# Score pairs spread among a step's products, in a two-layer attention and mixer kernel

## The chip, the cores and the metric

The kernel runs on one core of a Trainium2 chip. The metric is the device time of one execution in microseconds, the median over several runs. The engines are TensorE (PE in the profile, with its weight loads as PEld), VectorE (DVE), ScalarE (ACT), GpSimd (POOL) and SyncE (SP, which only issues DMAs here). TensorE writes to PSUM alone; DVE and ACT clear PSUM into SBUF, and POOL and the DMAs work on SBUF.

## The reference

For each of 8 batches, with 3200 rows, 256 columns of `v` and `u` and 64 of `z`:

```python
scores = (1.0 / S) * z @ z.T                 # 3200 x 3200
attn   = maximum(scores, 0) ** 2
x      = u * (attn @ v)                      # 3200 x 256

wq, wk = x @ w_q, x @ w_k                    # 3200 x 64
mixed  = (1 / sqrt(64)) * (wq @ wk.T) @ x    # computed as wq @ (wk.T @ x)
out    = maximum(mixed, 0) @ w_out
```

## The kernel before

**Tiles and groups.** A batch's 3200 rows are 25 tiles of 128. The output rows of the attention are worked on in seven groups: six of 512 rows and a last one of 128. A *score* is a tile of keys against a group: one matmul of 64 rows (`z` has 64 columns) by 512 columns. Two of them make a *pair*, one in the lower 64 partitions of the array and one in the upper, which run side by side, into one PSUM tile `sc` of two banks (`scores`, L275). Each pair is cleared by one instruction, `relu` and a scale into `g` (`first_stage`: DVE L289 or ACT L287), and squared by another into `at` in 16 bits (`second_stage`: ACT L298 or POOL L300). Scores are symmetric, so some `at` tiles are transposed by DMA (L317) into `tt` and serve a second group.

**Products.** The sum over keys of `at` against `v` goes to two PSUM banks, `acc0` and `acc1`, each holding two of a group's four row tiles (`second_product`). Its 128 key rows are also cut into two *lanes*, the lower and the upper 64 partitions. In pass one the lower lane works on one bank and the upper lane on the other; in pass two they have changed banks, so that two lanes never write one bank at once (`lanes`, L333 through `Item.emit`). Between the passes stands `swap_after`: a nop on TensorE that waits for the last matmul of each lane of pass one. `evened` pads a shorter lane with zeros. The last group of a batch but the last is *split*: it has one row tile, each lane has a bank for itself, and it needs no swap (`both_lanes`).

**Steps.** The main loop (`while groups`) runs 171 steps. A step scores up to three pairs, squares those of the step before (`waiting`), and multiplies some of the rows that were scored two steps before or kept from earlier. A step may *begin* a group (its accumulators start) or *close* it: then `gate` multiplies the sums with `u` (ACT copies one bank, L441; DVE takes the other, L442; POOL finishes, L444), and SP transposes the result for the mixer. Between the groups' work come pieces of the mixer: a step may *mix* (two matmuls `mx` at its head and two pairs in place of three), carry *keys* (`qk`: projections and heads), or a *projection* (`fo`, 512 output rows, then stored).

**Where the pairs stand.** A step that begins a group scores all its pairs at its head, but one less where it carries keys or a projection. Another step scores one pair at its head, or none where it mixes. The other pairs are `between_`: the program issues them all between the two passes, after the second squaring of ACT, ahead of the nop of the swap:

```python
firsts = [lanes(part, across, False) for part in parts]
...
for x in acts[1:]:
    second_stage(*x)
for p0 in between_:
    stage(p0, scores(p0))
...
for part, ends_ in zip(parts, firsts):
    swap_after(ends_)
    lanes(part, across, True)
```

Where a middle or closing step carries keys or a projection, pass one is: half of the products, the extra's first pass, the other half; then come the later pairs, the swap and second pass of the extra, and the swap and second pass of the products. In a beginning step the extra stands first.

**What orders the work.** The order is written out by hand: each engine takes its instructions in the order in which this loop issues them, and semaphores alone make them wait. The second pair of a step is cleared by ACT (the first in the step after a group's end), the others by DVE; in a step that mixes ACT clears the mix and DVE both pairs. Of the pairs of the step before, POOL squares the first, ACT the second, and a third is ACT's in even steps and POOL's in odd ones. PSUM tiles for `sc`, `mx`, `qk` and `fo` come from one pool of three (`pps`), `g` from seven.

Of the kernel before, what the change touches and what calls it, by code (L numbers as in the profile page):

```python
# [16 lines left out]
def kernel(  # L17
# [218 lines left out]
    for b in range(B):  # L236
        for gi in range(NG):
# [7 lines left out]
            else:  # L245
                odd = len(tiles) % 2
                order, rest = own[:odd], own[odd:]
                n_, m_ = len(near) // 2, (len(rest) + 1) // 2
                at_ = sorted(
                    [((i + 0.5) / max(n_, 1), near[2 * i : 2 * i + 2]) for i in range(n_)]  # L250
                    + [((i + 0.7) / max(m_, 1), rest[2 * i : 2 * i + 2]) for i in range(m_)]
                )
# [11 lines left out]
    def scores(p0):  # L264
        pair = tiles[p0 : p0 + 2]
        sc = ps_tile("sc")
        ats = [[], []]
        for h, (b, gi, tis) in enumerate(pair):
            w = widths[gi]
            half = h * dqk  # L270
            for i in range(W // w):
                ti = tis[min(i, len(tis) - 1)]
                ats[h].append((i * w, h, w, b, ti, starts[gi], half))
        for at, h, w, b, ti, gs, half in sorted(ats[0] + ats[1]):
            nc.tensor.matmul(  # L275
                out=sc[:, h, at : at + w],
                lhsT=zT[b][half : half + dqk, ds(z_at(b, h) + ti * P, P)],
                rhs=zT[b][half : half + dqk, ds(z_at(b, h) + gs, w)],
                start=True,
                stop=True,  # L280
            )
        return sc
# [11 lines left out]
    def second_stage(p0, g, on_act):  # L294
        at = pat.tile([P, 2 * W], FP16, tag="at", name="at")
        out = at[:].rearrange("p (a w) -> p a w", a=2)
        if on_act:
            nc.scalar.square(out=out, in_=g[:])  # L298
        else:
            nc.gpsimd.tensor_mul(out=out, in0=g[:], in1=g[:])  # L300
        blocks = []
        for h, (b, gi, tis) in enumerate(tiles[p0 : p0 + 2]):
            for i, ti in enumerate(tis):
                made[b, gi, ti] = (at, h * W + i * widths[gi])
            gj = group_of(tis[0])
            if is_turned(gi, gj):
                blocks.append((b, gi, gj, tis[0] - starts[gj] // P, 1, h * W, (h + 1) * W))
        if len(blocks) == 2 and blocks[0][:3] == blocks[1][:3] and blocks[1][3] == blocks[0][3] + 1:
            blocks = [blocks[0][:4] + (2, blocks[0][5], blocks[1][6])]
        for b, gi, gj, n0, nn, c0, c1 in blocks:  # L310
            if (b, gi, gj) not in turned:
                bufs = {1: 3, 2: 4, 4: 1}[gj - gi]
                turned[b, gi, gj] = ptt.tile(
                    [P, 4, 4, P], FP16, tag=f"tt{gj - gi}", name=f"tt{gj - gi}", bufs=bufs
                )
            out = turned[b, gi, gj][:].rearrange("p n j t -> p (n j) t")
            nc.sync.dma_start_transpose(out=out[:, 4 * n0 : 4 * (n0 + nn), :], in_=at[:, c0:c1])  # L317
# [7 lines left out]
    ALL, LOW, HIGH = slice(0, P), slice(0, P // 2), slice(P // 2, P)  # L325

    class Item:
# [4 lines left out]
        def emit(self, rows, start, stop):  # L332
            return nc.tensor.matmul(  # L333
                out=self.out, lhsT=self.lhsT(rows), rhs=self.rhs(rows), start=start, stop=stop
            )
# [6 lines left out]
    def width(i):  # L342
        n = 1
        for d in i.out.shape[1:]:
            n *= d
        return n
# [12 lines left out]
            items[-1:-1] = [z_] * (n // D or 1)  # L359
        return items  # L360

    def lanes(banks, across, second):
        todo, ends_ = [], {}
        for lane, rows in enumerate((LOW, HIGH)):
            at = 0
            for i in evened(banks, lane ^ across):
                todo.append((at, lane, i, rows))
                at += width(i)
        for _, lane, i, rows in sorted(todo, key=lambda x: x[:2]):
            ends_[lane] = i.emit(rows, i.start and not second, i.stop and second)  # L370
        return list(ends_.values())

    def both_lanes(banks):
        for low, high in zip(*banks):
            low.emit(LOW, low.start, low.stop)
            high.emit(HIGH, high.start, high.stop)

    def swap_after(ends_):
        ins = nc.tensor.nop()
        for earlier in ends_:  # L380
            tc.add_manual_dep(
                ins.ins,
                earlier.ins.name,
                mybir.DependencyInfo(mybir.DependencyClass.Sync, mybir.DependencyReason.DATA),
                reason="the lanes change banks",
            )
# [133 lines left out]
    def spread_heads(b):  # L520
        nc.scalar.copy(out=hss[b][dh:P, :], in_=hss[b][0:dh, :])
        nc.scalar.copy(out=hz[b % 2][dh:P, :], in_=hss[b][0:dh, :])
# [165 lines left out]
    keyed, keyed_at, to_turn, to_spread, asides = [], [-9], [], [], []  # L688
# [124 lines left out]
    def key_due(k):  # L813
# [10 lines left out]
            return False  # L824
        return since > 2

    made_by = []
    waiting = []
    produced = consumed = k = 0
    groups = [(b, gi) for b in range(B) for gi in range(NG)]  # L830
    left, steps, across = None, 0, False
    gate_pending = False
    while groups:
# [3 lines left out]
        n = 4 if k == 0 else 6  # L837
        mixing = None
# [6 lines left out]
        if mix_due(k):  # L845
            mixing = todo_mix.pop(0)
            mixed_at[0] = k
            mixing += (mix(*mixing),)
            n = 4
        n = min(n, NTILE - produced)  # L850
        pairs = list(range(produced, produced + n, 2))
        on_lanes = k >= 3 and len(pairs) + bool(mixing) >= 2
        keying = not mixing and key_due(k)
        begins = left is None
        projecting = not keying and todo_proj and groups[0] != (last, LASTG) and (
            begins or len(todo_proj) > 2 or len(groups) <= NG
        )
        heading = len(pairs)
        if on_lanes:
            heading = heading - bool(keying or projecting) if begins else 1 - bool(mixing)  # L860
        between_ = pairs[heading:]
        pairs = pairs[:heading]
        fresh = [(p0, scores(p0)) for p0 in pairs]
# [7 lines left out]
        def stage(p0, sc):  # L871
            on_act = len(staged) == act_pair and not mixing
            staged.append((p0, first_stage(p0, sc, on_act)))
# [15 lines left out]
        acts = [x for x in seconds if x[2]]  # L889
# [14 lines left out]
        b, gi = groups[0]  # L904
# [16 lines left out]
        closes = steps == 1  # L921
# [5 lines left out]
        rows_ = [t for _, _, tis in tiles[consumed : consumed + new] for t in tis]  # L927
# [7 lines left out]
        extra = None  # L935
# [6 lines left out]
        if on_lanes:  # L942
            split = is_split(b, gi)
            if extra and not all(extra[0]):
                for fn in whole(extra[0]):
                    fn()
                extra[1]()
                extra = None
            parts = [] if split else [banks]
            if extra and not begins and not split:  # L950
                n_ = len(banks[0]) // 2
                parts = [[bank[:n_] for bank in banks], extra[0], [bank[n_:] for bank in banks]]
            elif extra:
                parts.insert(0, extra[0])
            cut = len(rows_) // 4
            firsts = [lanes(part, across, False) for part in parts]
            if len(parts) == 3:
                parts, firsts = [extra[0], banks], firsts[1:]
            if split:
                both_lanes([bank[:cut] for bank in banks])  # L960
            for x in acts[1:]:
                second_stage(*x)
            for p0 in between_:
                stage(p0, scores(p0))
            if parts:
                across = not across
            for part, ends_ in zip(parts, firsts):
                swap_after(ends_)
                lanes(part, across, True)
                if extra and part is extra[0]:  # L970
                    extra[1]()
            if split:
                both_lanes([bank[cut:] for bank in banks])
        else:
            assert not is_split(b, gi)
            matmuls = whole(banks)
            cut = 10 if extra else 0
            if closes and (b, gi) == (last, LASTG):
                assert not extra
                cut = 20  # L980
                psg = [acc_tile(1, "xtx")[:, 0:D], ps_tile("xtx")[:, 0, 0:D]]
                extra = [], lambda: last_gram(last, LASTG - 1, psg)
            for fn in matmuls[:cut]:
                fn()
            if extra:
                for fn in whole(extra[0]):
                    fn()
                extra[1]()
            for x in acts[1:]:
                second_stage(*x)  # L990
            for fn in matmuls[cut:]:
                fn()
# [5 lines left out]
            left = None  # L998
        while to_spread:
            spread_heads(to_spread.pop(0))  # L1000
        waiting = staged
        k += 1

# [85 lines left out]
```

## Time and profile before

| | |
|---|---|
| runs | 799.5, 800.5, 802.95 us; median 800.5 |
| the profiled execution | 801.4 us |
| its span, first to last instruction | 799.6 us |
| mean granted TensorE clock | 0.997 |
| PE, PEld busy | 97%, 86% |
| DVE, ACT, POOL busy | 58%, 70%, 69% |
| DMA | 147.03 MB, 184 GB/s in the mean |

A row of the profile's groups names the line, the engine, the operation, the tiles written and read, their shapes and the count; then the busy time of the group, the mean of one in ns, the idle time of the engine just before them, and who ended most of it. A row of the timeline gives the start, the length, the engine and line, and in brackets the idle time of the engine ahead of it with its releaser; equal instructions that follow one another are merged (x24). A row of the waits gives who waited for whom, us in total, how many times and the longest. Ends of matmuls are modelled: one of 256 columns lasts 0.27 us in the records, though the next in its lane starts 0.11 us after it, so idle time of PE shorter than that does not show as idle.

### The profile page before, as it was taken

Reading aid. Unit: us, or ns where it says so; the run is one execution under the profiler, and the core shown is the slowest. Engines: PE = TensorE matmul, PEld = TensorE weight load, DVE = VectorE, ACT = ScalarE, POOL = GpSimd, SP = SyncE. Lnnn points to the kernel's source line nnn. Section 1 sums busy time; section 2 is a strip of 40 time slices with the busy share of each in tenths; the row PEclk is TensorE's granted clock in tenths of the full one; section 3 lists DMA queues with packets and bytes.
Section 4 is the critical chain, followed back from the end, with each engine's and each line's share of the span. In section 5 each row is a group of like instructions: output and inputs, shape, how many; then the busy total and the mean of one; then the engine's idle time right before and its main releaser. Section 6 shows DMA issues by size and latency. Waiting matters only on the chain. (4 is left out here: it accounts for less than half of the span.)

```text
span 799.6 us, 28394 instructions
## 1 busy us (share of the span) xinstructions
PE 773.6 (97%) x12590; PEld 683.9 (86%) x12590; DVE 465.8 (58%) x455; ACT 559.7 (70%) x656; POOL 553.2 (69%) x364
## 2 busy tenths in 40 slices
PE   7999999999999999999989999999999999999996
PEld 4878879998899988999879997999988898887984
DVE  5755576556655557455746457655575556664434
ACT  6776777877768776676767667758686877574565
POOL 7888698768666677765959658985677536866350
PEclk9999999999999999999999999999999999999999
DMA  8999799975999579994799949899499994987526
GB/s 156 179 218 200 132 204 185 189 178 121 211 218 203 126 181 210 207 241 128 172 212 228 225 123 165 230 187 256 119 207 200 220 222 94 187 186 162 157 58 256
DMA packets 276266, 147.03 MB, mean 184 GB/s; under 512 B 252080, under 2 KB 255664, under 8 KB 276144
## 3 DMA queue, kind: packets, MB, share of 16 engines
q1 hardware_dynamic: 275424, 143.33, 83.7%
q0 software_dynamic: 576, 1.64, 1.2%
q8 instruction: 98, 1.61, 0.8%
q14 instruction: 24, 0.20, 0.1%
q10 hardware_dynamic: 144, 0.26, 0.1%
HBM read 59.38 MB, written 26.21 MB: 107 GB/s over the span
## 5 line engine op out<-in xcount | busy, mean ns | idle before, releaser
L289 DVE TENSOR_SCALAR g<-sc 128x1024 f32<-128x1024 f32 x338 | 405.7, 1221 | 281.2 <-PE sc L275 253.0
L333 PE MATMUL acc<-v_sb,at 64*128 64x256 f16 (+1 forms) x7387 | 481.0, 270 | 3.6 <-POOL at L300 1.6
L300 POOL TENSOR_TENSOR at<-g 128x1024 f16<-128x1024 f32 x239 | 447.2, 1894 | 35.5 <-DVE g L289 35.3
L333 PEld LDWEIGHTS <-at 64*128 64x128 f16 (+1 forms) x7387 | 405.4, 94 | 51.0 <-issue 6.3
L298 ACT ACTIVATE at<-g 128x1024 f16<-128x1024 f32 x229 | 235.1, 1054 | 39.0 <-DVE g L289 38.1
L287 ACT ACTIVATE g<-sc 128x1024 f32<-128x1024 f32 x130 | 133.2, 1025 | 78.5 <-PE sc L275 77.0
L444 POOL TENSOR_TENSOR x_sb<-gt,u_sb 128x512 f16<-128x512 f32 x48 | 61.2, 1275 | 178.1 <-ACT gt L441 172.0
L333 PE MATMUL acc<-v_sb,tt 64*128 64x256 f16 (+1 forms) x2540 | 180.6, 269 | 0.0
L275 PE MATMUL sc<-zT 64*128 64x512 f16 (+1 forms) x1104 | 161.0, 347 | 5.6 <-ACT g L287 3.3
L333 PEld LDWEIGHTS <-tt 64*128 64x128 f16 (+1 forms) x2540 | 142.5, 94 | 3.3
L275 PEld LDWEIGHTS <-zT 64*128 64x128 f16 x1104 | 63.4, 94 | 14.7 <-issue 9.4
L578 ACT ACTIVATE rt<-mx 128x1024 f16<-128x1024 f32 x47 | 47.9, 1025 | 24.5 <-PE mx L557 22.5
L333 PE MATMUL fo<-wo,rt 64*128 64x256 f16 (+1 forms) x688 | 58.6, 271 | 2.2 <-DVE g L289 1.3
L639 ACT ACTIVATE fo<-fo 128x1024 f32<-128x1024 f32 (+2 forms) x44 | 43.6, 999 | 20.7 <-PE fo L333 20.4
L333 PE MATMUL qk<-x_sb,kx 64*128 64x256 f16 x368 | 54.6, 269 | 2.1 <-DVE g L289 2.0
L333 PEld LDWEIGHTS <-rt 64*128 64x128 f16 (+1 forms) x688 | 42.5, 95 | 14.7 <-issue 6.5
L441 ACT COPY gt<-acc 128x512 f32<-128x512 f32 x48 | 28.2, 587 | 31.3 <-PE acc L333 30.9
L442 DVE TENSOR_TENSOR x_sb<-acc,u_sb 128x512 f16<-128x512 f32 x48 | 33.1, 689 | 20.5 <-PE acc L333 18.4
L333 PEld LDWEIGHTS <-kx 64*128 64x128 f16 (+1 forms) x386 | 36.0, 94 | 7.1 <-DMA kx<-ql 0.9
L333 PE MATMUL qk<-xT_sb,wkq 64*128 64x512 f16 (+1 forms) x90 | 31.6, 376 | 1.0 <-DMA xT_sb<-x_sb 1.0
L479 ACT CAST qk<-qk 128x512 f16<-128x512 f32 x47 | 27.3, 582 | 7.1 <-PE qk L333 7.0
L333 PE MATMUL qk<-xT_sb,wqk 64*128 64x512 f16 (+1 forms) x94 | 30.0, 377 | 0.0
(79 smaller groups left out, 260.4 us busy)
## 6 DMA issues: line engine op xcount, KB each, us to landing
u_sb<-in_u_dram SPq DMA_DIRECT2D x48, 512.0 KB, 5.1
out_dram<-fo SPq DMA_DIRECT2D x45, 512.0 KB, 3.5
piece<-in_v_dram SPq DMA_DIRECT2D x42, 512.0 KB, 4.7
piece<-in_z_dram SPq DMA_DIRECT2D x7, 512.0 KB, 5.6
tt<-at SPq DMA_TRANSPOSE x162, 5.1
piece<-in_z_dram SPq DMA_DIRECT2D x7, 288.0 KB, 5.9
out_dram<-fo SPq DMA_DIRECT2D x5, 256.0 KB, 2.7
u_sb<-in_u_dram SPq DMA_DIRECT2D x8, 128.0 KB, 3.2
```

The source lines that it names most:

```text
L275: nc.tensor.matmul(out=sc[:, h, at : at + w], lhsT=zT[b][half : half + dqk, ds(z_at(b, h) + ti * P, P)], rhs=zT[b][half : half + dqk, ds(z ...
L287: nc.scalar.activation(out=g[:], in_=sc[:], func=RELU, scale=GSCALE)
L289: nc.vector.tensor_scalar(out=g[:], in0=sc[:], scalar1=0.0, scalar2=GSCALE, op0=AOP.max, op1=AOP.mult)
L298: nc.scalar.square(out=out, in_=g[:])
L300: nc.gpsimd.tensor_mul(out=out, in0=g[:], in1=g[:])
L333: return nc.tensor.matmul(out=self.out, lhsT=self.lhsT(rows), rhs=self.rhs(rows), start=start, stop=stop)
L441: nc.scalar.copy(out=upper[:], in_=accs[1][:])
L442: nc.vector.tensor_mul(out=x[:, 0:n], in0=accs[0][:, 0:n], in1=ug[:, 0:n])
L444: nc.gpsimd.tensor_mul(out=x[:, n : 2 * n], in0=upper[:], in1=ug[:, n : 2 * n])
L479: nc.scalar.copy(out=qks[b, gi][:, 0:gw], in_=out)
L578: nc.scalar.activation(out=out, in_=ps[:], func=RELU)
L639: nc.scalar.mul(out=flat_out[:, sl], in_=part, mul=FINAL_SCALE)
```

## The change

The lists of matmuls of a step are no longer issued at once. `lanes` and `both_lanes` return the instructions with their columns; the step collects pass one, the nops and pass two in one list `emits`, and `run` issues it, putting each later pair in when its share of all the step's columns has been issued. A share of 0.5 is the place between the passes as before; ACT's second squaring goes there too, ahead of a pair with the same share. The shares hang on the kind of step: `m` neither begins nor closes, `c` closes, `b` begins, `s` is split; `x` mixes, `k` carries keys, `p` a projection.

```diff
-    def lanes(banks, across, second):
-        todo, ends_ = [], {}
+    def lanes(banks, across, second, ends_):
+        todo = []
...
-        for _, lane, i, rows in sorted(todo, key=lambda x: x[:2]):
+        def emit(lane, i, rows):
             ends_[lane] = i.emit(rows, i.start and not second, i.stop and second)
-        return list(ends_.values())
+        return [
+            (width(i) / 2, lambda lane=lane, i=i, rows=rows: emit(lane, i, rows))
+            for _, lane, i, rows in sorted(todo, key=lambda x: x[:2])
+        ]
...
+    def run(emits, asides_):
+        total, done = sum(n for n, _ in emits), 0
+        asides_ = sorted(asides_, key=lambda x: x[0])
+        for n, fn in emits:
+            while asides_ and asides_[0][0] * total <= done:
+                asides_.pop(0)[1]()
+            fn()
+            done += n
+        for _, fn in asides_:
+            fn()
...
+    shares_of = {
+        "m": (0.0, 0.5, 0.5),
+        "mx": (0.12, 0.5, 0.5),
+        "mk": (0.0, 0.5, 0.5),
+        "mp": (0.25, 0.5, 0.5),
+        "c": (0.25, 0.5, 0.5),
+        "cx": (0.0, 0.5, 0.5),
+        "ck": (0.0, 0.5, 0.5),
+        "cp": (0.25, 0.5, 0.5),
+        "b": (0.5, 0.5, 0.5),
+        "bk": (0.5, 0.5, 0.5),
+        "bp": (0.5, 0.5, 0.5),
+        "s": (0.3, 0.3, 0.3),
+        "sx": (0.0, 0.3, 0.3),
+        "sk": (0.4, 0.3, 0.3),
+        "sp": (0.4, 0.3, 0.3),
+        "bx": (0.5, 0.5, 0.5),
+    }
...
             if split:
-                both_lanes([bank[:cut] for bank in banks])
-            for x in acts[1:]:
-                second_stage(*x)
-            for p0 in between_:
-                stage(p0, scores(p0))
+                emits += both_lanes([bank[:cut] for bank in banks])
             if parts:
                 across = not across
             for part, ends_ in zip(parts, firsts):
-                swap_after(ends_)
-                lanes(part, across, True)
+                emits.append((0, lambda ends_=ends_: swap_after(ends_.values())))
+                emits += lanes(part, across, True, {})
                 if extra and part is extra[0]:
-                    extra[1]()
+                    emits.append((0, extra[1]))
             if split:
-                both_lanes([bank[cut:] for bank in banks])
+                emits += both_lanes([bank[cut:] for bank in banks])
+            at_ = shares(begins, closes, split, len(between_))
+            todo = [(x, lambda p0=p0: stage(p0, scores(p0))) for x, p0 in zip(at_, between_)]
+            for x in acts[1:]:
+                todo.append((0.5 - 1e-6, lambda x=x: second_stage(*x)))
+            run(emits, todo)
```

The rest of the diff bounds two counts (`heading`, `n_`) and empties a list of side work once more at a step's end; in this program neither changes an instruction.

More of the change, by code (lines that the diff above doesn't have):

```diff
@@ L368, in lanes @@
                 at += width(i)
-        for _, lane, i, rows in sorted(todo, key=lambda x: x[:2]):
+        def emit(lane, i, rows):
             ends_[lane] = i.emit(rows, i.start and not second, i.stop and second)
-        return list(ends_.values())
+        return [
+            (width(i) / 2, lambda lane=lane, i=i, rows=rows: emit(lane, i, rows))
+            for _, lane, i, rows in sorted(todo, key=lambda x: x[:2])
+        ]
     def both_lanes(banks):
-        for low, high in zip(*banks):
-            low.emit(LOW, low.start, low.stop)
-            high.emit(HIGH, high.start, high.stop)
+        return [
+            (width(i) / 2, lambda i=i, rows=rows: i.emit(rows, i.start, i.stop))
+            for both in zip(*banks)
+            for i, rows in zip(both, (LOW, HIGH))
+        ]
+    def run(emits, asides_):
[8 more added lines that the diff above has]
+            fn()
     def swap_after(ends_):
@@ L825, in key_due, with shares @@
         return since > 2
+    shares_of = {
[16 more added lines that the diff above has]
+    }
+    def shares(begins, closes, split, n):
+        key = "s" if split else "b" if begins else "c" if closes else "m"
+        key += "x" if mixing else "k" if keying else "p" if projecting else ""
+        return shares_of[key][:n]
     made_by = []
@@ L860 @@
             heading = heading - bool(keying or projecting) if begins else 1 - bool(mixing)
+            heading = max(0, min(len(pairs), heading))
         between_ = pairs[heading:]
@@ L950 @@
             if extra and not begins and not split:
-                n_ = len(banks[0]) // 2
+                n_ = max(2, min(len(banks[0]) - 2, len(banks[0]) // 2))
                 parts = [[bank[:n_] for bank in banks], extra[0], [bank[n_:] for bank in banks]]
@@ L954 @@
                 parts.insert(0, extra[0])
-            cut = len(rows_) // 4
-            firsts = [lanes(part, across, False) for part in parts]
+            firsts = [{} for part in parts]
+            emits = []
+            for part, ends_ in zip(parts, firsts):
+                emits += lanes(part, across, False, ends_)
             if len(parts) == 3:
                 parts, firsts = [extra[0], banks], firsts[1:]
+            cut = len(rows_) // 4
             if split:
-                both_lanes([bank[:cut] for bank in banks])
-            for x in acts[1:]:
-                second_stage(*x)
-            for p0 in between_:
-                stage(p0, scores(p0))
+                emits += both_lanes([bank[:cut] for bank in banks])
             if parts:
@@ L1000 @@
             spread_heads(to_spread.pop(0))
+        while asides:
+            asides.pop(0)()
         waiting = staged
```

## The prediction, made before the run

> **What bounds the kernel now.** I read the page first, then the chain that ended last (its ten pieces lie in the last 12 us, so it says nothing of the body), then the waits of TensorE and of its weight loads, and at last the timeline around the places that those waits name.
>
> ```profile
> span 799.6 us, 28394 instructions
> PE 773.6 (97%) x12590; PEld 683.9 (86%) x12590; DVE 465.8 (58%) x455; ACT 559.7 (70%) x656; POOL 553.2 (69%) x364
> L289 DVE TENSOR_SCALAR g<-sc 128x1024 f32<-128x1024 f32 x338 | 405.7, 1221 | 281.2 <-PE sc L275 253.0
> L287 ACT ACTIVATE g<-sc 128x1024 f32<-128x1024 f32 x130 | 133.2, 1025 | 78.5 <-PE sc L275 77.0
> ```
>
> TensorE is the bound; DVE and ACT mostly wait for its scores. But a busy PE is no PE at its peak: a matmul's modelled end (0.27 us for 256 columns) hides any hole shorter than that, so I measure by starts. One step and its successor, TensorE and DVE:
>
> ```profile
> 198.53 0.40 PE L557 MATMUL mx<-qk,hs 64*128 64x512 f16 x2
> 198.74 1.50 PE L333 MATMUL acc<-v_sb,at 64*128 64x256 f16 x24
> 200.05 0.62 PE L275 MATMUL sc<-zT 64*128 64x512 f16 x4
> 200.48 1.50 PE L333 MATMUL acc<-v_sb,at 64*128 64x256 f16 x24
> 200.56 2.36 DVE L289 TENSOR_SCALAR g<-sc 128x1024 f32<-128x1024 f32 x2 [1.92 <-PE sc L275]
> 201.79 0.62 PE L275 MATMUL sc<-zT 64*128 64x512 f16 x4
> 202.97 0.61 PE L333 MATMUL fo<-wo,rt 64*128 64x256 f16 x8 [0.56 <-DVE g L289]
> ```
>
> Starts give the pitch: 24 product matmuls take 200.05 - 198.74 = 1.31 us, 12 pairs of 0.109; two score pairs 0.43; one 512-column pair (the mix) 0.21. The last step breaks it: its two score pairs at 201.79 should hand over at 202.22, and the projection starts at 202.97, 0.75 late. It wants the PSUM tile of the second of two pairs that were scored together at 200.05, and DVE clears them one behind the other, from 200.56 to 202.92. That is the hole the change can close.
>
> What it can win at most is what TensorE waits for evictions:
>
> ```profile
> PE sc L275 <- ACT g L287: 3.3, 4, 2.1
> PE qk L333 <- DVE g L289: 2.0, 3, 0.7
> PE fo L333 <- DVE g L289: 1.3, 2, 0.7
> PE sc L275 <- DVE g L289: 0.4, 2, 0.2
> PEld L333 <- POOL at L300: 4.3, 8, 1.1
> PEld L333 <- PE acc L333: 3.2, 10, 0.3
> POOL x_sb L444 <- ACT gt L441: 172.0, 45, 9.7
> ```
>
> Columns: total, times, longest. The first four are evictions, 7.0 us beyond the modelled ends, and with the hidden part more. The fifth is POOL's squaring, whose order the change does not touch; the sixth is the drain between passes, of which below; in the seventh POOL waits for a group's end.
>
> **The change part by part.** Nothing is added or removed: the same matmuls, the same 171 steps with the same rows. By the order of issue DVE, POOL and SP keep their sequences exactly, DMAs included; TensorE's and ACT's differ. Steps with two later score pairs put the first of them earlier: at the start of pass one (17 plain middle steps, 16 middle and 13 closing ones with keys, 10 closing ones that mix), at 0.12 (25 middle steps that mix) or at 0.25 (21 plain closing, 8 with a projection). The second stays at half. Steps that begin a group keep their one later pair at half, where it was: their holes behind the gate and their uncovered drains stay, at no gain.
>
> *(1) A mixing step before a beginning one, ten closing steps.* Both pairs go to DVE. Now the first is scored at 198.74, cleared from about 199.25 (0.51 after its start, as 200.56 stands to 200.05) to 200.43; the second is scored at 200.27 and cleared from 200.78 to 201.97; the projection may start from 202.22. The hole goes. It is as long as pass two is short:
>
> ```profile
> 529.12 0.61 PE L275 MATMUL sc<-zT 64*128 64x512 f16 x4
> 529.78 0.61 PE L333 MATMUL fo<-wo,rt 64*128 64x256 f16 x8
> 300.62 0.61 PE L275 MATMUL sc<-zT 64*128 64x512 f16 x4
> 301.93 0.27 PE L333 MATMUL qk<-x_sb,kx 64*128 64x256 f16 x1 [0.70 <-DVE g L289]
> 693.43 0.61 PE L275 MATMUL sc<-zT 64*128 64x512 f16 x4
> 694.60 0.27 PE L333 MATMUL qk<-x_sb,kx 64*128 64x256 f16 x1 [0.56 <-DVE g L289]
> ```
>
> Less 0.43 for two pairs: 0.23 after eight rows (seven such places), 0.88 after five (one), 0.74 after six (two, the first row quoted above with 0.75). 7 x 0.23 + 0.88 + 0.75 + 0.74 = 4.0 us. After five rows the new margin is 0.21 + 1.09 + 0.43 = 1.73 against 0.51 + 1.18 = 1.69, still no hole. Two more steps that mix, in the short split groups, follow a step whose own two evictions keep DVE full; nothing there.
>
> *(2) ACT behind a late DVE, two places.*
>
> ```profile
> 216.18 1.06 ACT L298 ACTIVATE at<-g 128x1024 f16<-128x1024 f32 x1 [1.00 <-DVE g L289]
> 217.14 1.03 ACT L137 CAST v_sb<-piece 128x1024 f16<-128x1024 f32 x1
> 218.08 1.02 ACT L287 ACTIVATE g<-sc 128x1024 f32<-128x1024 f32 x1
> 218.29 0.47 PE L275 MATMUL sc<-zT 64*128 64x512 f16 x2
> 219.14 0.39 PE L275 MATMUL sc<-zT 64*128 64x512 f16 x2 [0.38 <-ACT g L287]
> ```
>
> In a middle mixing step the second DVE result comes late, ACT's squaring of it waits 1.00, a cast and the next eviction stand behind it, and a score waits 0.85 - 0.21 = 0.64. With the pairs apart, the second result comes about a pitch of DVE (1.18) less one score pair (0.21) sooner, 0.97 > 0.64. Two such places: 1.3 us.
>
> *(3) Split groups.* Their one later pair moves from about 0.30 of the columns to 0.4.
>
> ```profile
> 183.19 0.82 PE L333 MATMUL acc<-v_sb,at 64*128 64x256 f16 x12
> 184.01 0.39 PE L275 MATMUL sc<-zT 64*128 64x512 f16 x2
> ```
>
> Six pairs of 0.109 end at 183.84; the score waits 0.17 for ACT. It comes 0.3 us later now, products run meanwhile: three places, 0.5 us. With the 0.4 of the fourth wait row (a middle step's third pair behind a late DVE) the gains are 4.0 + 1.3 + 0.5 + 0.4 = 6.2 us.
>
> *(4) The swap of the banks.* Between the passes a nop waits for pass one's last matmuls. Two score pairs (0.43) covered that; in the 73 steps without keys or projection (17 + 25 + 21 + 10) only one pair is left. Beginning steps show the bare drain: last product, and first products after it:
>
> ```profile
> 29.65 0.27 PE L333 MATMUL acc<-v_sb,at 64*128 64x256 f16 x1
> 29.98 0.28 PE L333 MATMUL acc<-v_sb,at 64*128 64x256 f16 x2
> ```
>
> 0.33 from start to start, where the pitch alone gives 0.09 after a balanced pair: 0.24 bare. One score pair takes 0.21 to 0.22 of it, so 0.02 stays; 73 x 0.02 = 1.5 us. Bounds: 0 if it fits; and by the sixth wait row the weight loads stand idle 0.32 at each of ten drains, which less 0.21 leaves 0.11, 8.0 us. I take the value from the starts, since the loads run ahead of their matmuls and part of their idling costs nothing. In the other 37 the extra's columns lie before the last pass-one products or the second extra pass covers them: 0.
>
> [...]
>
> *(5) ACT's order.* In 23 steps with two squarings on ACT, the step's own eviction now stands ahead of the second squaring. That delays a product operand by about 1.03 us (its L287 row). It is made in the step before the one that reads it, and a step as the one shown lasts 201.79 - 198.53 = 3.26 us, so I cost it at nothing; without that cover, 23 x 1.0 is the most.
>
> *(6) An early pair that must wait for its tile.* Matmuls go in order, so it would hold the pass. It takes a tile cleared by DVE about 1.7 after its scoring at the previous half, and comes 0.21 + pass two + 0.21 (and often an extra's 0.43) after it, 1.96 with eight-row steps (12 pairs give 1.31 for six rows, 1.74 for eight, so 2.2): free. Five-row steps are short of it by 0.2, but there the order of issue gives it the tile of an earlier pair. Nothing.
>
> Sum: -6.2 + 1.5 = -4.7 us. The profiled execution took 801.4 us (799.6 of span and 1.8 around it), so 796.7; it lies 0.9 above the median of the runs, 800.5, and against that I predict 795.8.
>
> **The rivals.**
>
> *Given back.* Products run earlier, and the next late thing stops them: POOL's squaring (the fifth wait row, 4.3 us at eight places) keeps its order and its pace. If it eats as much again as it has now, the sum is -6.2 + 1.5 + 4.3 = -0.4 and the time 800. For it speaks that POOL is 69% busy; against it the seventh row: POOL stands still at 45 group ends, 3.8 us each, until TensorE comes, so no backlog lasts beyond a group.
>
> *Slower: the swap is not covered by one pair.* If the drain begins anew behind the score pair, because the products' weights can't be loaded until the nop has passed, each of 73 swaps costs the bare 0.24: 17.5 - 6.2 = 11.3, 812. It decides from 0.14 a swap (10.2 us, a net loss of 4). Against it: with two pairs no hole stands at the swap (200.05 to 200.48 is exact pitch), so part of the drain does run beside scores.
>
> *More than the sum.* One hole hangs on a DMA:
>
> ```profile
> 400.03 1.04 ACT L137 CAST zr<-piece 128x1024 f16<-128x1024 f32 x1 [2.65 <-DMA piece<-in_z_dram]
> 402.05 0.61 PE L275 MATMUL sc<-zT 64*128 64x512 f16 x4 [2.11 <-ACT g L287]
> 402.80:406.20 3.40, 3.06 (x30) 2.53 (x31) 2.02 (x3) 3.14 (x4) 2.99 (x2) 0.50 1.43 174
> ```
>
> ACT's cast waits for the piece, an eviction stands behind the cast, TensorE waits 2.11 us, and then its granted clock is 0.50 for 3.4 us, another 1.7. The cast keeps its place in ACT's order, so I count nothing; but if the piece lands in time in the new rhythm, 3.8 more go: 792. The same kind of hole may as well open elsewhere.
>
> **How the numbers follow.** A difference of about 0.5%, 4 us, is what a measurement of this kernel can tell from no change. The sum's own case (792.5 to 799) has 0.55, of which 0.40 lies below 796.5 and 0.15 above it. More than the sum: 0.12, all faster. Given back: 0.22, of which 0.04 beyond 804.5. The uncovered swap: 0.11, of which 0.08 slower. That is faster 0.52, same 0.36, slower 0.12. From 791 to 802 lie the sum with both bounds of the swap, the rival above and the one given back; the rest of the uncovered swap and larger wins are left out.
>
> **What would show it.** In the profile after: L289's two-behind-each-other rows of DVE in mixing steps come apart; the waits of fo and qk for DVE g and of sc for ACT g shrink to below 3 us together; each swap's products start within 0.25 us of the score pair's start; the waits for POOL stay near 4. Wrong it would be if those swaps show 0.3 or more, if squarings on ACT (L298) come up as releasers of products, or if the DMA holes multiply.

## The result and the profile after

The changed kernel took 793.21 us (median of 4 executions, 793.14 to 794.13) against 801.27 (799.5 to 802.95) for the kernel before: a ratio of 0.9902, 95% interval 0.9878 to 0.9927. In the last series of experiments it took 794.89 (793.44 to 798.01) against 799.56 (798.55 to 801.87), a ratio of 0.9938, 0.9919 to 0.9957. So it is faster by 4.7 to 8.1 us; 795.8 had been predicted, and 791 to 802 as the range.

The page of the changed kernel, profiled in an execution of 793.18 us, beside which the one before had 801.4:

```profile
span 790.8 us, 28408 instructions
PE 769.5 (97%) x12590; PEld 658.3 (83%) x12590; DVE 470.4 (59%) x455; ACT 559.8 (71%) x656; POOL 552.6 (70%) x364
L289 DVE TENSOR_SCALAR g<-sc 128x1024 f32<-128x1024 f32 x338 | 411.3, 1222 | 265.0 <-PE sc L275 235.8
L287 ACT ACTIVATE g<-sc 128x1024 f32<-128x1024 f32 x130 | 133.0, 1023 | 41.0 <-PE sc L275 35.4
```

The work is the same; the span is 8.8 us shorter. DVE and ACT are as busy as before. ACT's idle time ahead of its evictions is 37 us less in the last row (78.5 before); ACT is not the bound, so that by itself counts for nothing. The waits of the changed kernel (who waited for whom, total, times, longest):

```profile
PEld L333 <- PE acc L333: 18.4, 75, 0.3
ACT at L298 <- DVE g L289: 16.2, 18, 1.6
ACT v_sb L137 <- DMA piece<-in_v_dram: 7.5, 7, 3.0
PEld L333 <- POOL at L300: 2.8, 4, 1.0
PE sc L275 <- ACT g L287: 1.6, 2, 1.2
PE qk L333 <- DVE g L289: 0.8, 2, 0.6
PE fo L333 <- DVE g L289: 0.7, 1, 0.7
```

TensorE's waits for evictions went from 7.0 us to 3.1, POOL's part from 4.3 to 2.8. The drains of the weight loads went the other way, from ten (3.2 us) to 75 (18.4 us): those are the swaps with one pair of cover. The step that the prediction began with, and its successor, in the timeline of the changed kernel:

```profile
198.36 0.38 PE L579 MATMUL mx<-qk,hs 64*128 64x512 f16 x2
198.58 0.38 PE L275 MATMUL sc<-zT 64*128 64x512 f16 x2
198.79 1.47 PE L333 MATMUL acc<-v_sb,at 64*128 64x256 f16 x24
199.07 1.23 DVE L289 TENSOR_SCALAR g<-sc 128x1024 f32<-128x1024 f32 x1 [0.75 <-PE sc L275]
200.10 0.38 PE L275 MATMUL sc<-zT 64*128 64x512 f16 x2
200.33 1.48 PE L333 MATMUL acc<-v_sb,at 64*128 64x256 f16 x24
200.52 1.23 DVE L289 TENSOR_SCALAR g<-sc 128x1024 f32<-128x1024 f32 x1 [0.23 <-PE sc L275]
201.65 0.59 PE L275 MATMUL sc<-zT 64*128 64x512 f16 x4
202.08 0.60 PE L333 MATMUL fo<-wo,rt 64*128 64x256 f16 x8
```

DVE clears the pairs at 199.07 and 200.52, and the projection starts at 202.08, 0.43 after 201.65: exact pitch, where 0.75 had been lost. The swap lies between 200.10 and 200.33, 0.23 where one pair's pitch is 0.21.

**The account.** I compared the start of every matmul of the two traces with the earliest that its lane's predecessor allows (0.109 us for 256 columns, 0.21 for 512) and listed what is left, place by place. The sums in the table are worked out from those lists, for the two profiled executions.

| | predicted | found |
|---|---|---|
| (1) holes ahead of ten beginning steps | -4.0 | -3.9 |
| the wait at the gate behind eight of them, 0.05 to 0.09 each | not counted | -0.5 |
| (2) ACT behind a late DVE, two places | -1.3 | -1.3 |
| (3) split groups, three places | -0.5 | -0.6 |
| the fourth wait row | -0.4 | -0.5 |
| (4) 73 swaps, by the lane that loses most | +1.5 | +2.6 |
| the hole at the cast of a z piece, with its clock | not counted | -2.2 |
| holes behind POOL's squaring, three of five; transposes of keys, two | not counted | -1.2 |
| some smaller ones, both signs | | -0.6 |

That is -8.2 of the -8.8 us of span.

### The profile page after: what moved, and what is told of

Same layout as the page of the kernel before. It is cut to its first block, busy times and chain, and to the rows that moved or that the text cites. A ratio compares the mean times of both kernels' runs of the same rounds, so it can differ in the third digit from the quotient of the medians.

```text
span 790.8 us, 28408 instructions
## 1 busy us (share of the span) xinstructions
PE 769.5 (97%) x12590; PEld 658.3 (83%) x12590; DVE 470.4 (59%) x455; ACT 559.8 (71%) x656; POOL 552.6 (70%) x364
## 5 line engine op out<-in xcount | busy, mean ns | idle before, releaser
L289 DVE TENSOR_SCALAR g<-sc 128x1024 f32<-128x1024 f32 x338 | 411.3, 1222 | 265.0 <-PE sc L275 235.8
L333 PEld LDWEIGHTS <-at 64*128 64x128 f16 (+1 forms) x7387 | 388.7, 94 | 68.4 <-PE acc L333 18.4
L275 PE MATMUL sc<-zT 64*128 64x512 f16 (+1 forms) x1104 | 168.2, 346 | 3.2 <-ACT g L287 1.6
L333 PEld LDWEIGHTS <-tt 64*128 64x128 f16 (+1 forms) x2540 | 135.4, 94 | 10.1
L275 PEld LDWEIGHTS <-zT 64*128 64x128 f16 x1104 | 60.0, 94 | 11.1 <-issue 3.5
```

The lines of the kernel that those rows point to most:

```text
L275: nc.tensor.matmul(out=sc[:, h, at : at + w], lhsT=zT[b][half : half + dqk, ds(z_at(b, h) + ti * P, P)], rhs=zT[b][half : half + dqk, ds(z ...
L289: nc.vector.tensor_scalar(out=g[:], in0=sc[:], scalar1=0.0, scalar2=GSCALE, op0=AOP.max, op1=AOP.mult)
L333: return nc.tensor.matmul(out=self.out, lhsT=self.lhsT(rows), rhs=self.rhs(rows), start=start, stop=stop)
```

## The experiments

The edits are to the table of shares, `m` middle, `c` closing, `x` mixing, and so on, unless a diff shows another line; each starts from the changed kernel but the last one. Ratios are to the kernel before, measured on the same chip.

**Which shares bring the gain.** Three kernels: the closing mixing steps put back; only the mixing steps' shares changed; only the others'.

```diff
-        "cx": (0.0, 0.5, 0.5),
+        "cx": (0.5, 0.5, 0.5),
```

> As the changed kernel, but in the ten steps that close a group and mix both score pairs stand between the passes again. My theory (the gain comes from the two evictions of a mixing step that no longer stand behind each other on DVE): the holes ahead of the following projections and keys come back, 3.7 us by the two traces, and ten swaps are covered again, 0.5 us: 793.2 + 3.2 = 796.4, and the profile shows fo and qk waiting for DVE at those ten places. Rival (the gain comes from scores spread evenly, whatever the step): ten of 118 moved pairs are worth a twelfth of 8 us, 794.

Measured: 797.71 us (796.46 to 801.18), ratio 0.9971, 0.9958 to 0.9985. The ten holes are back one by one. In its timeline, the same place:

```profile
200.25 0.59 PE L275 MATMUL sc<-zT 64*128 64x512 f16 x4
200.69 1.47 PE L333 MATMUL acc<-v_sb,at 64*128 64x256 f16 x24
200.75 2.36 DVE L289 TENSOR_SCALAR g<-sc 128x1024 f32<-128x1024 f32 x2 [2.06 <-PE sc L275]
202.00 0.59 PE L275 MATMUL sc<-zT 64*128 64x512 f16 x4
203.16 0.61 PE L333 MATMUL fo<-wo,rt 64*128 64x256 f16 x8 [0.57 <-DVE g L289]
```

203.16 - 202.00 - 0.43 = 0.73, the hole of before, with DVE's two evictions on end again. The time is 1.3 us above what theory (1) expected; against the changed kernel's two ratios it is 2.6 to 5.5 us, where 3.2 were expected. Its profiled execution was its longest (801.18) and has two holes of 1.7 us at pieces of z and v besides, so this trace shows the places and not the price.

```diff
-        "m": (0.0, 0.5, 0.5),
+        "m": (0.5, 0.5, 0.5),
...
-        "sk": (0.4, 0.3, 0.3),
+        "sk": (0.3, 0.3, 0.3),
```

> As the kernel before, but the steps that mix have the changed shares (0.12, or 0 where they close a group); every other later pair stands between the passes, as before. My theory: this alone holds nearly all of the gain of the evictions (3.7 at the closing ones, 1.3 at the two late scores on ACT, 0.4 at middle steps) and half of the swaps' cost (35 of 73, 1.0 us): 801.3 - 4.4 = 796.9, and up to 2.4 less if the hole at 402 us shrinks too. Rival (spreading as such): 37 of 118 pairs, 801.3 - 2.5 = 798.8.

Measured: 796.44 us (795.79 to 797.58), ratio 0.9948, 0.9929 to 0.9968, as expected. Its waits:

```profile
PE qk L333 <- DVE g L289: 0.8, 2, 0.6
PE fo L333 <- DVE g L289: 0.7, 1, 0.7
```

They equal the changed kernel's. The two places of ACT behind DVE (2) and the fourth row are gone too: each follows a mixing step.

```diff
-        "mx": (0.12, 0.5, 0.5),
+        "mx": (0.5, 0.5, 0.5),
...
-        "cx": (0.0, 0.5, 0.5),
+        "cx": (0.5, 0.5, 0.5),
...
-        "sx": (0.0, 0.3, 0.3),
+        "sx": (0.2, 0.2, 0.2),
```

> The complement: the steps that mix have both pairs between the passes, as in the kernel before, all other steps the changed shares. My theory: 38 swaps cost 0.7 us, the split groups win 0.5, the holes behind mixing steps all stay: 801.3 within 1 us (less, if the hole at 402 us shrinks by itself: then 799). Rival (spreading as such): 81 of 118 pairs, 801.3 - 5.5 = 795.8.

Measured: 799.78 us (798.63 to 802.57), ratio 0.9995, 0.9981 to 1.0009: nothing gained that can be told, and the second of the two expected values. At the z cast TensorE waits 0.92 us in place of 2.11 and keeps its clock (1.0 in the mean of the execution). The waits for DVE are close to those of before:

```profile
PE qk L333 <- DVE g L289: 2.2, 4, 0.7
PE fo L333 <- DVE g L289: 1.3, 2, 0.7
```

So the gain is that of the mixing steps' shares; the other kinds pay their swaps with the split groups and what happens at the z cast. The two parts give 0.9948 x 0.9995 = 0.994 together, which is the second measurement of the whole (0.9938) and not the first (0.9902).

**The price of a swap.** The second pair ahead of the end of pass one leaves the swap bare:

```diff
-        "c": (0.25, 0.5, 0.5),
+        "c": (0.25, 0.4, 0.4),
```

and the same in `m`, `mx` and `cx`.

> As the changed kernel, but in the 73 steps without keys or projection the second pair stands at 0.4 of the columns in place of 0.5, so that no score covers the wait between the passes. My theory: each of the 73 swaps shows the bare drain, 0.24 us in place of some 0.05: 793.2 + 73 x 0.19 = 807. Rival (the drain runs beside anything, the score pair was not what covered it): 793 to 795, since the pair only comes 0.3 us sooner to its eviction.

Measured: 806.76 us (806.61 to 808.94), ratio 1.0082, 1.0061 to 1.0103: slower than before, as the theory had it. A swap in its timeline:

```profile
221.52 0.38 PE L333 MATMUL acc<-v_sb,tt 64*128 64x256 f16 x4
221.97 1.05 PE L333 MATMUL acc<-v_sb,at 64*128 64x256 f16 x16
```

Four matmuls are two pairs of 0.109; 221.97 - 221.52 - 0.22 = 0.23 is bare. The starts show two sizes in the two kernels. Of the 67 swaps that can be told in the changed kernel's trace, 54 have lanes that end pass one together: 0.24 bare, and 0.02 to 0.03 behind a pair. In the other 13 one lane ends about 0.09 ahead of the other, and both start again together: the lane that was ahead stands 0.31 bare and 0.10 behind a pair, the other one about 0.02 behind a pair. One pair covers 0.21 of either. By the lane that loses most that is 2.6 us in all, 0.036 in the mean of 73 swaps, where the expectation has some 0.05. The rival of an uncovered swap is refuted: a pair does run in the drain.

```diff
-        "m": (0.0, 0.5, 0.5),
+        "m": (0.5, 0.5, 0.5),
...
-        "c": (0.25, 0.5, 0.5),
+        "c": (0.5, 0.5, 0.5),
```

> As the changed kernel, but the 38 plain middle and closing steps have both later pairs between the passes again, as before the change. My theory (their shares win nothing, their swaps cost): the residues of 38 swaps go, 1.0 us by the two traces, 792.2. Rival (an earlier pair in plain steps also frees ACT and DVE ahead of the next group's beginning): 794 to 795.

Measured: 794.77 us (792.74 to 796.34), ratio 0.9913, 0.9889 to 0.9936. The swaps' 1.0 us went from the trace, but the time didn't follow: 792.2 had been expected, and 794 to 795 by the rival, so this run alone does not refute it. Two of its waits:

```profile
ACT v_sb L137 <- DMA piece<-in_v_dram: 13.8, 6, 4.0
PEld L333 <- PE acc L333: 9.7, 38, 0.3
```

Half the drains are gone (75 to 38), and ACT waits longer for pieces of v (7.5 to 13.8 us); at three steps that comes to TensorE as holes of 0.9, 1.4 and 0.7, since an eviction stands behind the cast. The late pieces are the subject of the last group, whose fourth kernel tries these shares again.

**Split groups and ACT's order.**

```diff
-        "sk": (0.4, 0.3, 0.3),
-        "sp": (0.4, 0.3, 0.3),
+        "sk": (0.3, 0.3, 0.3),
+        "sp": (0.3, 0.3, 0.3),
```

> As the changed kernel, but the one later pair of the five split steps with keys or a projection stands at 0.3 of the columns, its old place. My theory: the waits of that pair for ACT come back, 0.4 to 0.6 us in all: 793.7. Rival (they were made by a late ACT that the other shares have freed): 793.2, without the waits.

Measured: 796.08 us (794.87 to 798.26), ratio 0.9933, 0.9911 to 0.9955. The time is further off than the part can explain, but its waits are back: here six pairs from 95.64 end at 96.29 and the score starts at 96.49.

```profile
95.64 0.83 PE L333 MATMUL acc<-v_sb,at 64*128 64x256 f16 x12
96.49 0.39 PE L275 MATMUL sc<-zT 64*128 64x512 f16 x2
```

```diff
-                todo.append((0.5 - 1e-6, lambda x=x: second_stage(*x)))
+                todo.append((-1.0, lambda x=x: second_stage(*x)))
```

> As the changed kernel, but ACT's second squaring is issued ahead of everything between the passes and so ahead of the early pair's eviction, as it stood before the change; only ACT's order differs, in 23 steps. My theory (the order costs nothing and wins nothing, because both have slack of a step): 793.2 within 0.8. Rival (part of the gain comes from evictions that no longer stand behind a squaring that waits for DVE): 794.5 or more, with more waits of sc for ACT g.

Measured: 795.5 us (793.95 to 797.48), ratio 0.9922, 0.99 to 0.9944, between the two measurements of the changed kernel, though above the 793.2 within 0.8 that was expected. Putting ACT's second squaring first wins nothing that can be told. Of the 2.4 us that its trace loses against the changed kernel's, 1.6 lie at two late transfers: near 67 us ACT waits 4.7 us for a transpose of z, near 82 us DVE waits 2.7 us for a piece of `u`.

**The hole at the z cast, and late pieces.** In the changed kernel's timeline ACT stands still until the piece lands, casts it, and only then clears the tile that the next score wants; the last row is the stretch behind it, whose fields are the busy times of the engines, then PEclk (1.00), DMA share and GB/s:

```profile
396.53 1.04 ACT L137 CAST zr<-piece 128x1024 f16<-128x1024 f32 x1 [2.62 <-DMA piece<-in_z_dram]
397.48 1.02 ACT L287 ACTIVATE g<-sc 128x1024 f32<-128x1024 f32 x1
398.55 0.61 PE L275 MATMUL sc<-zT 64*128 64x512 f16 x4 [1.25 <-ACT g L287]
...
399.00:403.00 4.00, 3.52 (x61) 3.17 (x60) 2.53 (x4) 3.44 (x5) 3.30 (x3) 1.00 1.34 184
```

Before, the wait was 2.11 and the clock half for 3.4 us. The first kernel moves the z casts alone one step later (a second line, not shown, keeps each cast on its engine):

```diff
-        due(k + 3, lambda: asides.append(cast))
+        due(k + (4 if src is z else 3), lambda: asides.append(cast))
```

> As the changed kernel, but ACT's and POOL's casts of the two pieces of z are issued one step later (on the same engine as before), so that no eviction stands behind a cast whose piece has not landed. My theory (the hole ahead of the fourth batch's second group is the landing of that piece, and the changed kernel shows only what is left of it): the 1.41 us for ACT and the 0.66 us behind it go, 793.2 - 2.0 = 791.2. Rival (the hole is made by the order of the scores; the cast is late by chance): 793, with the same wait at another row.

Measured: 803.33 us (800.38 to 804.85), ratio 1.0016, 0.9999 to 1.0033: a miss by 12 us. The hole at the z cast did go, but eleven others opened, of 0.5 to 1.9 us. Waits of this kernel, of ACT and POOL for pieces of v, and of SP's queue:

```profile
ACT v_sb L137 <- DMA piece<-in_v_dram: 26.5, 17, 4.4
POOL v_sb L137 <- DMA piece<-in_v_dram: 11.3, 8, 2.4
SPq L133 <- POOL zr L137: 19.0, 4, 5.2
```

In the changed kernel the last one was:

```profile
SPq L133 <- POOL zr L137: 4.9, 3, 4.1
```

L133 issues a piece's load. A z piece that is cast later holds its buffer longer, the next load waits for it (19.0 us in place of 4.9), and what SP issues after it waits behind that load: ACT's waits for pieces of v went from 7.5 to 26.5 us. So the loads of v have to move too:

```diff
-        due(k + 3, lambda: asides.append(cast))
+        due(k + (4 if src is z else 3), lambda: asides.append(cast))
...
-                at = k + (7 + 5 * i // 3 if b == 0 else 4 + 2 * i)
+                at = k + (8 + 5 * i // 3 if b == 0 else 5 + 2 * i)
```

(with the parity that picks the cast's engine turned, so that each cast keeps its engine). The changed kernel itself was run beside it:

> The changed kernel once more, as the measure for the others on the same chip. Both theories: 793.2 us, ratio to the kernel before 0.988 to 0.993; the step that waits for the cast of the z piece loses about 2.2 us, and the v pieces leave ACT waiting for 7 to 8 us in all, little of it on the path.

Measured: 794.89 us, ratio 0.9938 as told above, a little outside the expected 0.988 to 0.993.

> The changed kernel with the casts of z one step later and the loads and casts of v one step later too, so that the v loads no longer stand in the queue behind a load that waits for a buffer. Theory (what is late next are late landings, and the v pieces were late in the run with only z moved because z held the buffers): the hole at the z cast, 2.2 us, goes and the v holes don't open: 791 us. Rival (the landings are late wherever the loads are put, because the queue or the buffers are short): the holes come back at other steps, 793 us or more.

Measured: 791.99 us (791.18 to 792.83), ratio 0.9897, 0.9879 to 0.9915, which does not overlap that of the changed kernel on the same chip. In its timeline TensorE goes through, and the cast comes three rows of ACT's later:

```profile
396.18 1.25 PE L333 MATMUL acc<-v_sb,at 64*128 64x256 f16 x20
397.27 0.59 PE L275 MATMUL sc<-zT 64*128 64x512 f16 x4
...
399.81 1.04 ACT L137 CAST zr<-piece 128x1024 f16<-128x1024 f32 x1
```

20 matmuls are 1.09 us: the score starts on pitch. One hole of 0.77 opened at a later step, where ACT's squaring waits for a late DVE, with an eviction behind it.

> The run with z and v later, and the shares of the middle and closing steps back at one half, so that their uneven swaps, 1.0 us in all, go. Theory: both gains add up, 790 us. Rival: the landings move to other steps again, 793 us or more.

Measured: 791.15 us (790.55 to 794.06), ratio 0.9895, 0.9877 to 0.9914: no better than the one before that can be told, though its swaps are cheaper. So the early pair of the plain steps neither wins nor costs anything that a time shows. Its profiled execution was its longest, 794.06, and has one large hole of its own: POOL waits for `u`, TensorE for the gate, and the clock falls (PEclk 0.67).

```profile
82.44 1.27 POOL L466 TENSOR_TENSOR x_sb<-gt,u_sb 128x512 f16<-128x512 f32 x1 [3.93 <-DMA u_sb<-in_u_dram]
83.15 1.24 PE L333 MATMUL acc<-v_sb,at 64*128 64x256 f16 x11 [2.22 <-DVE x_sb L464]
...
82.00:86.00 4.00, 2.85 (x30) 2.55 (x31) 2.96 (x3) 4.00 (x5) 3.56 (x3) 0.67 1.19 175
```

The last kernel is that of before, with the two edits of the loads:

> The kernel before with the same later casts of z and later loads and casts of v, shares untouched. Theory (the hole at the z cast is worth 4 us before, since the clock halves behind it, and it has its own cause): 797 us. Rival (the hole is not taken away by the later loads, or another opens): 800 to 801 us.

Measured: 796.62 us (795.99 to 802.96), ratio 0.9972, 0.9953 to 0.999. The later pieces are worth 2 to 3 us with either order of the scores, and the two gains are nearly independent: 0.9938 x 0.9972 = 0.991, against 0.9897 measured with both. In its waits the scores' wait for ACT is down from 3.3:

```profile
PE sc L275 <- ACT g L287: 0.6, 2, 0.3
```

## Why the prediction was right

The time came out 2.6 us below the prediction in the first measurement and, by the ratio of the second (0.9938 x 800.5 = 795.5), 0.3 below. The sum of -4.7 was right for its reason in its largest part, and two errors of it worked against each other.

- **Step (1)** holds: the ten holes come to 4.3 us by the starts, 0.37 of which stayed, so 3.9 for 4.0, and it is shown, since putting back that one share brings all ten holes back. One of its claims failed: after five rows there should have been no hole, and this is where the 0.37 stayed. The step assumed that DVE starts 0.51 after the scoring. In the changed kernel's timeline:

```profile
293.77 3.92 POOL L300 TENSOR_TENSOR at<-g 128x1024 f16<-128x1024 f32 x2 [1.92 <-DVE g L289]
297.28 0.38 PE L275 MATMUL sc<-zT 64*128 64x512 f16 x2
298.13 1.23 DVE L289 TENSOR_SCALAR g<-sc 128x1024 f32<-128x1024 f32 x1 [0.52 <-POOL at L300]
298.61 0.59 PE L275 MATMUL sc<-zT 64*128 64x512 f16 x4
299.41 0.27 PE L333 MATMUL qk<-x_sb,kx 64*128 64x256 f16 x1 [0.21 <-DVE g L289]
```

  DVE starts 0.85 after the scoring, and the profile puts its wait down to POOL's squaring, that is, to a `g` tile: what is late next, the rival "given back" at one place. Elsewhere POOL gave nothing back; three of its five holes closed.
- **Step (2)** and the fourth row: 1.3 and 0.5 as sized. They belong to the mixing steps' shares, as the second kernel shows.
- **Step (3)**: 0.6 for 0.5. Putting the shares back brings the waits back; the time alone would not have told.
- **Step (4)** had the right mechanism and a term that was too small: 2.6 for 1.5. I took every swap as one whose lanes end together; those cost 0.02 to 0.03 as said. The 13 with uneven lanes cost one lane 0.10, and for a lane that ends late my sum had no term.
- **Step (5)**: the kernel with the squaring first was not faster, so the later squaring costs nothing that can be told.
- **Step (6)**: no wait of a score for DVE's eviction is left in the waits of the changed kernel (0.4 us, the fourth wait row, before).
- **The rival "more than the sum"** came in part: the hole at the z cast shrank by 2.2 of the 3.8 us, with the clock kept (1.00 over the next 4 us). The prediction had named it, counted it at nothing and called it open to luck, and it is that: the changed kernel's second profile has 2.8 us there against 2.2 in the first. So the first measurement owes that part to a landing that no step of the sum foresaw. The price was a little high: by the starts of the two traces the 3.4 us at half clock cost about 1.35 us and not 1.7. **The uncovered swap** and **given back** are refuted, the first by the swaps' size, the second, but for the one place above, by POOL's waits.
- **The signs.** Two came out otherwise than named: the three kinds of waits for evictions shrank to 3.1 and not below 3, and POOL's waits to 2.8. One sign of being wrong came up in part: at 12 of the uneven swaps the products start 0.3 us or a little more behind the score pair. The mechanism stands all the same, since the 54 even ones start after 0.23 to 0.24.

What stays open is the size of the gain between 4.7 and 8.1 us. The traces suggest a cause: in its second profile the changed kernel loses 0.56 at one step, where ACT casts a late piece of v, that the first doesn't lose, and the kernels that differ from it little (795.5, 796.1, 794.8 us) differ in the traces at late transfers most of all: pieces of v, z and `u`, and a transpose of z. Why one lands later in one execution wasn't shown.

## What to carry to other kernels

Where one engine clears two tiles that were produced together, the second tile's user waits for both; producing them half a step apart cost no work here (12590 matmuls in either page), and it paid where that user follows closely, so move only those (the mixing steps alone gave a ratio of 0.9948, the others 0.9995). When a filler is moved out of a drain, price the drain from the last matmul of either lane: the lane that ended first stands still longest (0.10 us behind a pair, where the other had about 0.02). And look at what stands in the same in-order engine behind a wait for a load: a cast one step later gained 3 us, but only when the loads behind it in the queue were moved as well; alone it cost 6 to 9.

## What the runs showed of the chip

**The clock after a wait.** The same hole, at the z cast, was followed by a lower clock in some executions and not in others, and between 1.72 and 1.76 us its length does not decide it. In the kernel with only the mixing shares changed, TensorE waits 1.72 us and the granted clock over the next 4 us is 0.69:

```profile
400.21 0.61 PE L275 MATMUL sc<-zT 64*128 64x512 f16 x4 [1.72 <-ACT g L287]
...
400.40:404.40 4.00, 3.52 (x37) 2.60 (x35) 2.15 (x3) 3.70 (x6) 3.03 (x2) 0.69 1.38 204
```

In the second profile of the changed kernel it waits 1.76 us, and the clock stays at 1.00:

```profile
399.53 0.61 PE L275 MATMUL sc<-zT 64*128 64x512 f16 x4 [1.76 <-ACT g L287]
...
399.90:403.90 4.00, 3.52 (x60) 3.09 (x58) 2.45 (x4) 3.52 (x6) 3.22 (x3) 1.00 1.38 185
```

The matmuls in the stretch are 37 against 60. After 2.11 us (before) the clock fell as well, to 0.50 for 3.4 us, and after 2.22 us (the wait for `u` in the kernel with later pieces and plain shares), to 0.67 over 4 us; after 1.25 us (the changed kernel's first profile) it stayed at 1.00.

**So of two waits of 1.72 and 1.76 us the shorter one was followed by a lower clock and the longer one was not; those of 2.11 and 2.22 us both were.** What decides it at that length was not shown. Where it fell, the wait cost more than itself: in the kernel before, 2.27 us of lost starts and about 1.35 us at half clock. One late piece of z counted for nearly as much as all ten holes of step (1) together.
